# An attention and feed-forward kernel: own score buffers for the first block's head pairs, shared with the first weight tiles, and ten memsets on another engine

## The chip, the cores and the metric

The kernel runs on one core of one Trainium2 chip. A core has a matrix engine (TensorE, PE in the profile, its weight loads PEld), a vector engine (VectorE, DVE), a scalar engine (ScalarE, ACT), a general engine (GpSimd, POOL) and a queue that here issues all transfers (SyncE, SP). Matrix results land in PSUM, everything else lies in SBUF. The metric is the device time of one execution in microseconds (us), as a median of runs.

## What is computed

The reference, cut to what matters; the inputs are float32, and q, k, v and w_in are scaled so that the softmax is far from flat.

```python
# q, k, v: (8 batches, 8 heads, 576 positions, 64); w_in (512, 2048), w_out (2048, 512)
scores = np.matmul(q, k.transpose(0, 1, 3, 2)) / np.sqrt(D)
mask = (rel >= 0) & (rel < 64)            # rel: position of q less position of k
scores = np.where(mask, scores, -1e9)
attn = softmax(scores)
x = np.matmul(attn, v)                    # heads side by side: (4608, 512)
h = x @ w_in
g = np.maximum(h, 0.0) + np.log1p(np.exp(-np.abs(h)))   # softplus
out = g @ w_out                           # (4608, 512)
```

## The kernel before

The 4608 tokens are worked off in 12 blocks of 384 (three tiles of 128). The first two blocks in `ORDER` are the first of their kind, called block 0 and block 1 here, and have an attention of their own in float32 (`by_pe`); the ten others split their operands into high and low parts. A block's attention goes over four pairs of heads. For a pair, SP loads q and k (L204, L206; `kbd` is a block-diagonal key tile whose zeros are memset once) and v (L226, L229); PE multiplies (L254); DVE scales, masks and takes the minimum (L265) into the score buffer `st` and merges the two ends of the window (L271); ACT takes six exponentials (L275); DVE normalises (L280, L281, L283); PE transposes (L290) and multiplies with v (L347); ACT and DVE leave the result as a high and a low part `x` (L352, L353). `st` has two buffers, so pair 2 takes the buffer of pair 0.

The feed-forward part goes over 16 slices of 128 hidden units. `ffn_up` multiplies x with a slice of w_in in twelve products (L401), ACT and DVE form the softplus in L405 to L407 and L409 and split it into `g` (L411, L412), and `ffn_down` adds the slice's nine products with w_out (L422) into three PSUM banks. Block 0 runs slices 0 to 7 first and leaves its partial sums in a DRAM tile `part` (L441, L442); block 1 then runs all 16 slices, block 0 the other eight, and blocks 2 to 11 follow. Block 2's attention lies beside block 1's feed-forward part.

The weights arrive as 64-bit words, 8 KB per partition for a slice of both matrices (1 MB), and are converted on the chip by `load_w`: a transfer into `raws` (L166), ACT (L170), three DVE instructions (L171, L172, L173) in `ws`, two ACT casts that give the high parts (L176) and two POOL subtractions that give the low parts (L177). The buffers of `raws` and `ws` are in the pool `late` under the tags `spare0` to `spare7`; slices 0 to 11 take them in turn. Slices 12 to 15 go through half tiles `raw` and `wh` instead; `raw` is also the buffer through which the partial sums leave.

The order of the work is set twice. `CONVERT`, `BASE`, `PACE` and `STG0` are due times, by which the program emits stages: a pair of block 0 takes its eight stages at `BASE[0] + PACE[0] * hp` plus an offset of `STG0`, so the loads of q and k at -104.5, -99.5, -94.5 and -89.5, and the normalisation and transposes at -96, -91, -86 and -81; the weights of slice f are emitted at `CONVERT[f]`. Then a scheduler places the emitted instructions on each engine by its own timing model, in another order than emitted where it finds that one ready first. From due time 100 on PE's order alone is the emitted one. Each engine, and SP's queue of transfers, works in order.

Of the kernel before, what the change touches and what calls it, by code (L numbers as in the profile page):

```python
# [8 lines left out]
F32 = mybir.dt.float32  # L9
# [6 lines left out]
P = 128  # L16
TB = 384
NJ = TB // P
WIN = 64
BIG = 1.0e9  # L20
CH = 64
# [1 line left out]

SPLIT = 8
DOWN = 5.5
CONVERT = (-104, -98, -93, -88, -6, -3, 0, 3, 6, 8, 11, 13, 16, 18, 21, 24)
BASE = (-100, -10, 24)
PACE = (5, 4, 7)
STG0 = (-4.5, 0.5, 1, 2, 3, 4, 7, 8)
# [10 lines left out]
def window_attention_softplus_ffn(  # L40
# [24 lines left out]
    nc = tc.nc  # L65
# [13 lines left out]
    att = ctx.enter_context(tc.tile_pool(name="att", bufs=1))  # L79
# [12 lines left out]
    NE = NF // 2  # L92
    w_first = [[cpool.tile([P, NE, DM], F32R, name=f"w{m}{i}") for i in range(2)] for m in range(2)]
    w_last = {}

    def spare(k, shape, dtype, name):
        return late.tile(shape, dtype, name=name, tag=f"spare{k}")

    def weight(m, i, f):

        if f < NE:
            return w_first[m][i][:, f, :]
        k = (f - NE) // 4
        if (m, i, k) not in w_last:
            w_last[m, i, k] = spare(4 * k + 2 * m + i, [P, 4, DM], F32R, f"w{m}{i}{k}")
        return w_last[m, i, k][:, f % 4, :]


    W = CH + P
# [2 lines left out]

    kbd_s = [att.tile([P, 2, CH + TB], F32, name="kbd", tag=f"k{i}") for i in range(2)]
    for t in kbd_s:
        nc.gpsimd.memset(t[D:P, 0, :], 0.0)
        nc.gpsimd.memset(t[0:D, 1, :], 0.0)
        nc.gpsimd.memset(t[0:D, 0, 0:CH], 0.0)
        nc.gpsimd.memset(t[D:P, 1, 0:CH], 0.0)

    v13 = cpool.tile([P, NCH, 2, 2, D], BF16, name="v13")  # L120
    v_ts = [att.tile([P, 2, NJ, P], F32, name="v_t", tag=n) for n in ("nat", "tr")]
    for t in v_ts:
        nc.gpsimd.memset(t[0:CH, 0, 0, :], 0.0)

# [23 lines left out]
    def load_w(f):  # L150


        if f < NE + 4:
            k = (0, 4, 2, 6)[f % 4] if f < NE else (4, 6)[f % 2]
            parts = [(spare(k, [P, 2, DM], w_words.dtype, "raws"), spare(k + 1, [P, 2, DM], F32, "ws"), 0, 2)]
        else:
            parts = [
                (
                    ff.tile([P, 1, DM], w_words.dtype, name="raw"),
                    att.tile([P, 1, DM], F32, name="wh", tag=("v_in", "v12")[m]),  # L160
                    m, m + 1,
                )
                for m in range(2)
            ]
        for raw, w, m0, m1 in parts:
            nc.sync.dma_start(raw, w_words[f][:, m0:m1, :])  # L166
            words = raw.bitcast(U32).rearrange("p m (n two) -> p two m n", two=2)
            low, high = words[:, 0, :, :], words[:, 1, :, :]
            wb = w.bitcast(U32)
            nc.scalar.activation(w, high.bitcast(F32), AF.Abs, scale=REBIAS)  # L170
            nc.vector.tensor_scalar(wb, wb, 3, None, ALU.logical_shift_left)  # L171
            nc.vector.scalar_tensor_tensor(wb, high, 0x80000000, wb, ALU.bitwise_and, ALU.bitwise_or)  # L172
            nc.vector.scalar_tensor_tensor(wb, low, 29, wb, ALU.logical_shift_right, ALU.bitwise_or)  # L173
            for m in range(m0, m1):
                hi, lo = [weight(m, i, f) for i in range(2)]
                nc.scalar.copy(hi, w[:, m - m0, :])  # L176
                nc.gpsimd.tensor_tensor(lo, w[:, m - m0, :], hi.bitcast(F32), ALU.subtract)  # L177
# [5 lines left out]
    def attention(g, hp):  # L183
# [59 lines left out]
            nc.vector.tensor_tensor(k_lo, k_in, k_hi.bitcast(F32), ALU.subtract)  # L243
        yield

        st = att.tile([P, 2, NJ, W], F32, name="st", bufs=2)
        mn = att.tile([P, 2, NJ], F32, name="mn", bufs=2)
        sm = att.tile([P, 2 * NJ], F32, name="sm", bufs=2)
        for j in range(NJ):
# [12 lines left out]
            t = ORDER[g] * NJ + j  # L262
# [192 lines left out]
    for g in range(NB):  # L455
        for hp in range(NP):
            if g < 3:
                base = BASE[g] + PACE[g] * hp
            else:
                base = 2 * NF * (g - 1) + SHP * hp + SH  # L460
            stages = attention(g, hp)
            for at in STG if g >= 2 else STG0:
                events.append((base + at, lambda stages=stages: next(stages, None)))
    loaded = 0
    for n, (g, f, first, last) in enumerate(steps):
        if f == loaded:
            events.append((CONVERT[f], lambda f=f: load_w(f)))
            loaded += 1
        events.append((2 * n + 0.5, lambda g=g, f=f: ffn_up(g, f)))
        events.append((2 * n + DOWN, lambda step=steps[n]: ffn_down(*step)))  # L470
# [52 lines left out]
```

## Time and profile before

| | us |
|---|---|
| median of three runs | 1030.87 (1030.74 to 1031.98) |
| the profiled execution | 1030.02 |
| its span, first to last instruction | 1028.2 |
| PE busy | 974.8 (95%) |
| DVE busy | 802.6 (78%) |
| ACT busy | 742.0 (72%) |
| POOL busy | 61.8 (6%) |

The profiled execution's own time is 1.8 us more than its span, for what lies around the instructions, and 0.85 less than the median. The shares are means over the whole span. POOL works only in the first fifth of it, and PE's idle time lies in its first sixth for the most part, so the rows further down are of that part.

### The profile page before, as it was taken

The numbers are of one execution on the slowest core, as the hardware profiler recorded it, in microseconds if no ns is written. First come the engines' busy times: TensorE is split into PE (matmuls) and PEld (weight loads), VectorE is DVE, ScalarE is ACT, GpSimd is POOL, SyncE is SP. The second block draws the span as 40 slices with busy tenths as digits, with TensorE's granted clock in tenths as the row PEclk, the third lists the DMA queues.
The fourth block names the chain that finished last, engine by engine and source line by source line (L and its number), as shares of the span: only waits on it lengthen the run. The fifth ranks groups of instructions, "written<-read, shape, count | busy, mean of one in ns | idle before, by whom it ended". The sixth has DMA issues, their size and how long they took to land.

```text
span 1028.2 us, 16614 instructions
## 1 busy us (share of the span) xinstructions
PE 974.8 (95%) x5888; PEld 859.1 (84%) x5888; DVE 802.6 (78%) x1775; ACT 742.0 (72%) x1705; POOL 61.8 (6%) x56
## 2 busy tenths in 40 slices
PE   4559889999999999999999999999999999999998
PEld 2337778988888998998899899899989899889997
DVE  6998587797987888878878878878878887874332
ACT  5467477787877788778778778778878877865443
POOL 5365020000000000000000000000000000000000
PEclk8679989999999999999999999999999999999999
DMA  8662253375554456444444534534634635521000
GB/s 295 229 219 71 88 149 83 83 186 123 126 121 114 113 114 130 117 113 116 131 103 117 140 91 118 151 83 113 164 83 113 161 86 104 141 49 32 31 1 31
DMA packets 203155, 119.05 MB, mean 116 GB/s; under 512 B 130880, under 2 KB 195136, under 8 KB 201536
## 3 DMA queue, kind: packets, MB, share of 16 engines
q1 hardware_dynamic: 203072, 118.00, 45.4%
q8 instruction: 46, 0.75, 0.3%
q14 instruction: 37, 0.30, 0.1%
HBM read 76.28 MB, written 10.22 MB: 84 GB/s over the span
## 4 chain that ended last, share of the span: by engine, by line
PE 85%; DVE 9%; DMA 2%; ACT 1%; issue 1%; SPq 1%; DVEq 0%; ACTq 0%
PE ps_o L422 37%; PE ps_h L401 37%; PE ps_a L376 5%; PE ps_a L258 5%; DVE ws L172 2%; DVE ws L173 1%; DVE st L265 1%; DVE st L283 1%; DMA raws<-in_w_words_dram 1%; DVE ws L171 1%; DVE st L271 0%; DMA tr<-nat 0%; ACT st L275 0%; PE ps_a L254 0%; DVE sm L280 0%
## 5 line engine op out<-in xcount | busy, mean ns | idle before, releaser
L401 PE MATMUL ps_h<-x,w 128*128 128x384 f32 x2304 | 445.3, 340 | 7.6 <-ACT x L352 3.9
L422 PE MATMUL ps_o<-w,g 128*128 128x512 f32 x1728 | 435.5, 395 | 0.0
L401 PEld LDWEIGHTS ps_h<-x,w 128*128 128x128 f32 x2304 | 402.6, 189 | 22.5 <-ACT x L352 5.2
L422 PEld LDWEIGHTS ps_o<-w,g 128*128 128x128 f32 x1728 | 318.0, 188 | 57.7 <-ACT g L411 0.3
L405 ACT ACTIVATE u<-ps_h 128x384 f32<-128x384 f32 x192 | 93.9, 490 | 121.8 <-PE ps_h L401 118.8
L409 DVE SCALAR_TENSOR_TENSOR u<-ps_h,u 128x384 f32<-128x384 f32 x192 | 106.4, 554 | 70.5 <-ACT u L407 69.2
L275 ACT ACTIVATE st<-st,mn 128x128 f32<-128x128 f32 x288 | 111.9, 390 | 19.3 <-DVE st L271 19.3
L412 DVE TENSOR_TENSOR g<-u,g 128x384 fp32r<-128x384 f32 x192 | 106.6, 555 | 10.5 <-ACT g L411 8.6
L265 DVE CUSTOM_DVE_ANT_0 st<-ps_a,mask 128x192 f32<-128x192 f32 x216 | 69.4, 351 | 57.9 <-PE ps_a L258 45.4
L407 ACT ACTIVATE u<-u 128x384 f32<-128x384 f32 x192 | 100.3, 523 | 4.2
L406 ACT ACTIVATE u<-u 128x384 f32<-128x384 f32 x192 | 100.7, 526 | 3.2
L258 PE MATMUL ps_a<-k,q_hl 128*128 128x192 f32 x480 | 76.5, 283 | 0.0
L376 PEld LDWEIGHTS <-v 128*128 128x128 bf16 x1088 | 56.1, 98 | 22.9 <-issue 21.8
L376 PE MATMUL ps_a<-tr,v 128*128 128x128 bf16 (+1 forms) x1088 | 72.0, 213 | 0.2
L258 PEld LDWEIGHTS ps_a<-k,q_hl 128*128 128x128 f32 x480 | 66.6, 192 | 4.1 <-issue 0.5
L411 ACT CAST g<-u 128x384 fp32r<-128x384 f32 x112 | 57.0, 509 | 14.2 <-DVE u L409 13.5
L306 ACT CAST nat<-st 128x768 bf16<-128x768 f32 x40 | 33.2, 831 | 40.0 <-DVE st L304 40.0
L275 ACT ACTIVATION_READ_ACCUMULATOR st<-st,mn 128x1 f32 x288 | 53.9, 187 | 0.0
L381 ACT COPY xf<-ps_a 64x384 f32<-64x384 f32 x80 | 38.1, 477 | 20.3 <-PE ps_a L376 19.2
L283 DVE TENSOR_TENSOR st<-st,sm 128x768 f32<-128x768 f32 x48 | 47.6, 991 | 1.5
L382 DVE TENSOR_TENSOR xf<-ps_a,xf 64x384 f32<-64x384 f32 x80 | 43.9, 548 | 5.2 <-ACT xf L381 4.0
L325 DVE TENSOR_TENSOR v_in<-v_in,v 128x896 f32<-128x896 f32 x40 | 43.5, 1086 | 4.7 <-ACT v L324 4.7
(80 smaller groups left out, 868.0 us busy)
## 6 DMA issues: line engine op xcount, KB each, us to landing
k_in<-in_kT_dram SPq DMA_DIRECT2D x80, 224.0 KB, 3.9
v_in<-in_v_dram SPq DMA_DIRECT2D x80, 224.0 KB, 3.6
q_in<-in_qT_dram SPq DMA_DIRECT2D x84, 192.0 KB, 4.1
raws<-in_w_words_dram SPq DMA_DIRECT2D x12, 1024.0 KB, 6.0
out_dram<-raw SPq DMA_DIRECT2D x12, 512.0 KB, 2.8
raw<-in_w_words_dram SPq DMA_DIRECT2D x8, 512.0 KB, 4.3
out_dram<-raw SPq DMA_DIRECT2D x12, 256.0 KB, 2.6
v_t<-in_v_dram SPq DMA_DIRECT2D x16, 96.0 KB, 3.8
```

Of the source, the lines that this page charges most:

```text
L258: mm(spv[:, hh, :], q_hl[:, hh, js], part[:, hh, kc], start=(hh == 0 and i == 0), stop=(hh == 1 and i == 1), skip_group_check=True,)
L265: nc.vector.tensor_tensor_reduce(st[:, hh, j, :], spv[:, hh, :], m, QSCALE, 3.0e38, ALU.add, ALU.min, mn[:, hh, j : j + 1])
L275: nc.scalar.activation(sv[:, i, 0:P], sv[:, i, 0:P], AF.Exp, bias=mn[:, hh, j : j + 1], scale=-1.0, accum_out=sm[:, i : i + 1])
L283: nc.vector.tensor_tensor(pn, pn, sm.unsqueeze(2).to_broadcast([P, 2 * NJ, P]), ALU.mult)
L376: mm(av[:, osl], (v13 if s else v12)[:, c, hh, :, :], src, start=(i == 0), stop=(i == len(passes) - 1), skip_group_check=True,)
L401: mm(hv, weight(0, a, f)[:, c * P : (c + 1) * P], x[b][c], start=(i_mm == 0), stop=(i_mm == 3 * NC - 1))
L405: nc.scalar.activation(u, hv, AF.Abs)
L406: nc.scalar.activation(u, u, AF.Exp, scale=-1.0)
L407: nc.scalar.activation(u, u, AF.Ln, bias=1.0)
L409: nc.vector.scalar_tensor_tensor(gf, hv, 0.0, u, ALU.max, ALU.add)
L412: nc.vector.tensor_tensor(gt[1], gf, gt[0].bitcast(F32), ALU.subtract)
L422: mm(ops[g][j], gt[a][:, js], weight(1, b, f), start=(first and i == 0), stop=(last and i == 2),)
```

## The change

It does three things. The ten memsets of `kbd` and `v_t` go from POOL to DVE. In block 0, each pair's score buffer is now a tile `st0` of its own, placed under the tags `spare0`, `spare4`, `spare2` and `spare6`, which the words of slices 0 to 3 take afterwards. And the due times of the first four weight slices go from -104, -98, -93 and -88 to -95.5, -90.5, -85.5 and -80.5, half a unit behind the normalisation and the transposes of the pair whose buffer they take.

```diff
-CONVERT = (-104, -98, -93, -88, -6, -3, 0, 3, 6, 8, 11, 13, 16, 18, 21, 24)
+CONVERT = (-95.5, -90.5, -85.5, -80.5, -6, -3, 0, 3, 6, 8, 11, 13, 16, 18, 21, 24)
...
+    FIRST = (0, 4, 2, 6)
...
-        nc.gpsimd.memset(t[D:P, 0, :], 0.0)
-        nc.gpsimd.memset(t[0:D, 1, :], 0.0)
-        nc.gpsimd.memset(t[0:D, 0, 0:CH], 0.0)
-        nc.gpsimd.memset(t[D:P, 1, 0:CH], 0.0)
+        nc.vector.memset(t[D:P, 0, :], 0.0)
+        nc.vector.memset(t[0:D, 1, :], 0.0)
+        nc.vector.memset(t[0:D, 0, 0:CH], 0.0)
+        nc.vector.memset(t[D:P, 1, 0:CH], 0.0)
...
-        nc.gpsimd.memset(t[0:CH, 0, 0, :], 0.0)
+        nc.vector.memset(t[0:CH, 0, 0, :], 0.0)
...
-            k = (0, 4, 2, 6)[f % 4] if f < NE else (4, 6)[f % 2]
+            k = FIRST[f % 4] if f < NE else (4, 6)[f % 2]
...
-        st = att.tile([P, 2, NJ, W], F32, name="st", bufs=2)
+        if g == 0:
+
+            st = spare(FIRST[hp], [P, 2, NJ, W], F32, "st0")
+        else:
+            st = att.tile([P, 2, NJ, W], F32, name="st", bufs=2)
```

Since the scheduler decides, the order itself shows what moved. The line numbers after the change are 2 higher up to L238 and 6 higher from L260 on. SP's queue from its start before (`raws` takes a whole slice's words, `k_in` and `q_in` hold q, `kbd` holds k):

```order
L204 DMA k_in_124<-in_qT_dram 128x384
L206 DMA kbd_89<-in_kT_dram 64x384 x2
L166 DMA raws_128<-in_w_words_dram 128x1024
L229 DMA v_t_100<-in_v_dram 64x128
L226 DMA v_t_100<-in_v_dram 128x2x128
L226 DMA v_t_100<-in_v_dram 64x3x128 x2
L204 DMA q_in_143<-in_qT_dram 128x384
L206 DMA kbd_90<-in_kT_dram 64x384 x2
L166 DMA raws_158<-in_w_words_dram 128x1024
```

And after, from the second pair's v on:

```order
L231 DMA v_t_101<-in_v_dram 64x128
L228 DMA v_t_101<-in_v_dram 128x2x128
L228 DMA v_t_101<-in_v_dram 64x3x128 x2
L206 DMA k_in_187<-in_qT_dram 128x384
L208 DMA kbd_89<-in_kT_dram 64x384 x2
L206 DMA q_in_259<-in_qT_dram 128x384
L208 DMA kbd_90<-in_kT_dram 64x384 x2
L168 DMA raw_983<-in_w_words_dram 128x512
L168 DMA raw_985<-in_w_words_dram 128x512
L168 DMA raws_172<-in_w_words_dram 128x1024
```

The first whole slice (`raws_128`, now `raws_172`) goes from the fourth transfer to behind q and k of all four pairs and behind two half tiles of slice 12. DVE from the end of pair 1's scores before:

```order
L271 TENSOR_TENSOR st_202<-st_202 128x6x64
L171 TENSOR_SCALAR ws_159<-ws_159 128x1024
L280 TENSOR_SCALAR sm_149<-sm_149 128x6
L172 SCALAR_TENSOR_TENSOR ws_159<-raws_158,ws_159 128x1024
L281 RECIPROCAL sm_149<-sm_149 128x6
L173 SCALAR_TENSOR_TENSOR ws_159<-raws_158,ws_159 128x1024
L283 TENSOR_TENSOR st_147<-st_147,sm_149 128x6x128
L280 TENSOR_SCALAR sm_204<-sm_204 128x6
L281 RECIPROCAL sm_204<-sm_204 128x6
L171 TENSOR_SCALAR ws_223<-ws_223 128x1024
L283 TENSOR_TENSOR st_202<-st_202,sm_204 128x6x128
```

And after:

```order
L277 TENSOR_TENSOR st0_191<-st0_191 128x6x64
L286 TENSOR_SCALAR sm_138<-sm_138 128x6
L287 RECIPROCAL sm_138<-sm_138 128x6
L289 TENSOR_TENSOR st0_136<-st0_136,sm_138 128x6x128
L286 TENSOR_SCALAR sm_193<-sm_193 128x6
L297 COPY pt_161<-ps_a_167 128x384
L287 RECIPROCAL sm_193<-sm_193 128x6
L289 TENSOR_TENSOR st0_191<-st0_191,sm_193 128x6x128
L173 TENSOR_SCALAR wh_984<-wh_984 128x512
```

The conversions have gone from between the steps of the two softmaxes; the first that follows is of a half tile. DVE in block 1's feed-forward part, from the 15th to the 18th end of a softplus (u), before:

```order
L409 SCALAR_TENSOR_TENSOR u_1326<-ps_h_1313,u_1326 128x384
L304 TENSOR_TENSOR st_1378<-st_1378,nat_1502 128x6x128
L311 COPY nat_1502<-nat_1502 128x12x64
L412 TENSOR_TENSOR g1_1332<-u_1326,g0_1331 128x384
L310 TENSOR_TENSOR nat_1502<-st_1378,nat_1502 128x12x64
L409 SCALAR_TENSOR_TENSOR u_1364<-ps_h_1351,u_1364 128x384
L412 TENSOR_TENSOR g1_1370<-u_1364,g0_1369 128x384
L409 SCALAR_TENSOR_TENSOR u_1429<-ps_h_1416,u_1429 128x384
```

And after, from shortly ahead of the 16th to the 17th:

```order
L418 TENSOR_TENSOR g1_1332<-u_1326,g0_1331 128x384
L310 TENSOR_TENSOR st_1545<-st_1545,nat_1721 128x6x128
L317 COPY nat_1721<-nat_1721 128x12x64
L331 TENSOR_TENSOR v_in_1774<-v_in_1774,v12_1921 128x896
L415 SCALAR_TENSOR_TENSOR u_1364<-ps_h_1351,u_1364 128x384
L335 COPY v13_99<-v12_1921 64x14x64
L286 TENSOR_SCALAR sm_1766<-sm_1766 128x6
L287 RECIPROCAL sm_1766<-sm_1766 128x6
L289 TENSOR_TENSOR st_1764<-st_1764,sm_1766 128x6x128
L316 TENSOR_TENSOR nat_1721<-st_1545,nat_1721 128x12x64
L334 TENSOR_TENSOR v13_99<-v_in_1774,v12_1921 64x14x64
L418 TENSOR_TENSOR g1_1370<-u_1364,g0_1369 128x384
```

Instructions of block 2's attention (names with st, nat, v_in, v12, v13) that stood behind these softplus ends stand ahead of them now.

## Rows read from the trace of the kernel before

**Rows 1.** Busy time of the engines by stretch of the span: start and end in us, length, then busy us and instructions of each engine, TensorE's granted clock as a share of full speed, busy share of the DMA engines, GB/s.

```profile
0.00:7.56 7.56, 3.06 (x5) 1.85 (x6) 0.00 (x1) 1.28 (x1) 6.51 (x24) 1.00 0.70 213
7.56:69.56 62.00, 32.55 (x166) 20.31 (x164) 60.32 (x117) 34.41 (x86) 29.78 (x17) 0.72 0.75 253
69.56:123.67 54.11, 47.07 (x264) 38.12 (x265) 40.85 (x89) 34.21 (x90) 18.64 (x12) 0.94 0.27 82
123.67:134.94 11.27, 5.67 (x41) 4.70 (x39) 5.40 (x11) 5.13 (x18) 0.00 (x0) 0.85 0.65 218
134.94:160.00 25.06, 23.16 (x114) 20.21 (x114) 24.75 (x56) 21.69 (x47) 6.84 (x4) 0.93 0.59 139
160.00:219.00 59.00, 58.77 (x360) 52.46 (x361) 43.12 (x98) 45.71 (x109) 0.00 (x0) 1.00 0.40 95
...
300.00:500.00 200.00, 200.00 (x1258) 179.47 (x1257) 167.45 (x384) 156.79 (x358) 0.00 (x0) 1.00 0.52 120
```

The columns of engines are PE, PEld, DVE, ACT and POOL.

**Rows 2.** PE's waits in the first 100 us: PE's line, the engine and line waited for, us in total, times, the longest.

```profile
PE ps_a L290 <- DVE st L283: 16.2, 3, 10.6
...
PE ps_o L254 <- DVE x L353: 4.8, 1, 4.8
```

**Rows 3.** The chain of work that ended last, in order of time, around the end of the first pass: start, us, what.

```profile
124.13 0.59 ACT raw L441
124.75 3.61 DMA part<-raw
128.38 3.58 DMA raw<-in_w_words_dram
132.04 0.67 ACT wh L170
133.19 0.70 DVE wh L172
133.91 0.69 DVE wh L173
```

**Rows 4.** The first instruction of L409, from DVE's timeline: start, us, engine, line, what.

```profile
78.79 0.55 DVE L409 SCALAR_TENSOR_TENSOR u<-ps_h,u 128x384 f32<-128x384 f32 x1
```

**Rows 5.** DVE's timeline in two stretches in which its instructions follow each other without a gap; a price is the distance from one start to the next.

```profile
81.42 0.34 DVE L265 CUSTOM_DVE_ANT_0 st<-ps_a,mask 128x192 f32<-128x192 f32 x1
...
81.69 0.35 DVE L265 CUSTOM_DVE_ANT_0 st<-ps_a,mask 128x192 f32<-128x192 f32 x1
...
81.97 0.68 DVE L171 TENSOR_SCALAR ws<-ws 128x1024 uint32<-128x1024 uint32 x1
82.57 0.54 DVE L412 TENSOR_TENSOR g<-u,g 128x384 fp32r<-128x384 f32 x1
83.04 1.21 DVE L173 SCALAR_TENSOR_TENSOR ws<-raws,ws 128x1024 uint32<-128x1024 uint32 x1
84.17 0.54 DVE L412 TENSOR_TENSOR g<-u,g 128x384 fp32r<-128x384 f32 x1
...
150.16 0.17 DVE L280 TENSOR_SCALAR sm<-sm 128x6 f32<-128x6 f32 x1
150.36 0.19 DVE L281 RECIPROCAL sm<-sm 128x6 f32<-128x6 f32 x1
150.59 0.96 DVE L283 TENSOR_TENSOR st<-st,sm 128x768 f32<-128x768 f32 x1
151.46 0.55 DVE L412 TENSOR_TENSOR g<-u,g 128x384 fp32r<-128x384 f32 x1
```

**Rows 6.** POOL's subtractions in the first 135 us, by line and form: count, busy us, mean ns of one, idle time before them and what ended it.

```profile
L177 POOL TENSOR_TENSOR w<-ws,w 128x512 fp32r<-128x512 f32 x24 | 41.9, 1768 | 42.1 <-ACT w L176 42.1
```

**Rows 7.** The tile `raws`, by line: count, duration in ns (least, median, most), first and last start; and the time from issue to landing of its transfers.

```profile
L170 ACT ACTIVATE ws<-raws x12: 1106/1139/1166, 9.2 to 79.7; 128x1024 f32<-128x1024 f32 x12
L172 DVE SCALAR_TENSOR_TENSOR ws<-raws,ws x12: 1212/1669/2294, 11.5 to 85.1; 128x1024 uint32<-128x1024 uint32 x12
...
DMA to landing us min/median/max: 4.8/6.0/11.0
```

**Rows 8.** The timeline of the first 12 us: POOL's first memset of `kbd`, the first transfer of words, POOL's first mask, PE's products of pair 0, POOL's last mask, DVE's first score reduction, PE's products of pair 1.

```profile
0.73 0.47 POOL L115 MEMSET kbd<- 64x448 f32 x1 [0.29 <-POOLq L509]
...
2.43 0.59 SPq L166 DMA_DIRECT2D raws<-in_w_words_dram  x1
...
3.52 0.26 POOL L129 MEMSET mask<- 128x192 bf16 x1
...
4.50 4.18 PE L254 MATMUL ps_a<-kbd,k_in 128*128 128x384 f32 x6 [4.50 <-DMA kbd<-in_kT_dram]
...
7.24 0.20 POOL L145 MEMSET mask_b<- 64x128 bf16 x1
...
7.56 0.36 DVE L265 CUSTOM_DVE_ANT_0 st<-ps_a,mask 128x192 f32<-128x192 f32 x1 [7.56 <-POOL mask_b L145]
...
11.40 3.58 PE L254 MATMUL ps_o<-kbd,q_in 128*128 128x384 f32 x6 [2.72 <-DMA kbd<-in_kT_dram]
```

**Rows 9.** The timeline of the softmaxes of pairs 0 and 1: two of ACT's exponentials that follow each other, DVE's two multiplications.

```profile
13.66 0.39 ACT L275 ACTIVATE st<-st,mn 128x128 f32<-128x128 f32 x1
...
14.04 0.39 ACT L275 ACTIVATE st<-st,mn 128x128 f32<-128x128 f32 x1
...
20.65 2.03 DVE L283 TENSOR_TENSOR st<-st,sm 128x768 f32<-128x768 f32 x1
...
25.52 0.94 DVE L283 TENSOR_TENSOR st<-st,sm 128x768 f32<-128x768 f32 x1
```

**Rows 10.** The chain of work again, in block 1's feed-forward part: the products of three groups in a full stretch.

```profile
174.99 2.13 PE ps_h L401 x12
177.11 2.08 PE ps_o L422 x9
...
183.47 2.10 PE ps_h L401 x12
```

## The prediction

> **What bounds the kernel now.** I read the busy time by stretch first, since the page's shares mix a front of some 160 us with 870 us in which PE is full. From 0 to 134.94 us VectorE (DVE) is busy 0.00 + 60.32 + 40.85 + 5.40 = 106.6 us and idle 28.4 us; from 160 to 219 us PE is busy all but 0.2 us of 59, and from 300 to 500 all of it [rows 1]. So only the front can change, and the change touches only the front. There PE's long waits are for DVE: 16.2 us for the softmax's multiplication (L283) and 4.8 us for an x (L353) [rows 2]. The chain says the same: between the end of the first FFN pass (L441) and the last x of block 1 (L353 at 134.94) it runs through the spilled partial sums, the reload of `raw` and DVE's conversion of a half weight tile, which stands ahead of that x on DVE [rows 3].
>
> DVE's idle time lies in four places: 7.56 us at the start, 1.68 us up to 69.56 (the last x of block 0), 13.26 us up to 123.67 (the first L441), 5.87 us up to 134.94 [rows 1]. The third is the prize: there PE works off the first pass and DVE has nothing ready, having converted ten weight tiles before PE had a first slice finished (first L409 at 78.79 [rows 4]).
>
> **The change, part by part.** Prices of DVE instructions are spacings of instructions that follow each other without a gap [rows 5]: L171 0.60, L172 and L173 1.13 each where nothing disturbs (2.86 for a conversion of a whole tile), 0.275 for a score reduction, 0.47 for L409, L412, L353 and their like; of a softmax, L280 0.20, L281 0.23 and the multiplication L283 0.87.
>
> Counted with these along the order, DVE's work up to the last x of block 1 is the same before and after: 12 conversions 34.3, 48 reductions 13.2, eight times L271, L280, L281, L283, L291 and L353 together 21.7, eight slices' L409 and L412 7.5, half tiles 8.0 and the rest 2.2, 86.9 us. The trace spends 106.6, so 19.7 us are stretching. I put it down to POOL's subtractions (24 of 1.77 us beside these conversions [rows 6]): L172 takes 1.21 at least and 2.29 at most [rows 7]. Both orders run the same subtractions beside the same conversions, so I keep 19.7. The Trainium skill (SBUF — State Buffer, Who interferes with whom) says that a VectorE instruction with two SBUF inputs and a GpSimd one that reads SBUF exclude each other, and that the second waits for the whole of the first. The trace bears out the direction; were all 24 waits whole, they would be 42 us and not 19.7, and the sum below would lose 23, which L172's longest row, 1.08 above its shortest, speaks against.
>
> *The memsets.* POOL's ten take from 0.73 to 3.52, and its masks from there until 7.44, when DVE starts [rows 8]. Without the ten, the masks are ready 2.8 earlier, at 4.7. Then PE is late next: its first products begin at 4.50, when the keys have landed, and take 4.18 for six, 1.4 for the pair of a tile, so DVE starts near 6.0, not 7.56: 1.6 saved. The trace has no memset on DVE; between half of POOL's price and twice it (1.4 to 5.6) they end at 2.1 to 6.3; I take POOL's price, 3.5, inside DVE's wait, and the long end costs 0.3.
>
> *Weights after the scores.* SP now issues both first heads' loads and v before any weight tile. The second pair's keys landed at 11.40 behind 1 MB of words issued at 2.43 [rows 8]; now near 9. The softmaxes of pairs 0 and 1 meet neither conversions nor POOL: pair 0's scores end near 9.3, its six exponentials (0.38 apart [rows 9]) near 12.3, pair 1's near 15.6, the two multiplications at 14.5 and 17.8, where they end at 22.7 and 26.5 now [rows 9]. In those 8 us DVE has 4.4 of work: idle 3.5, and about 1 for the first half tile. The first weight's load waits for pair 0's transposes at 16.1, and with 6.0 to landing [rows 7] and ACT's 1.1 DVE can convert from 23.5; by then it is still at its 13th us of counted work, near 24.7, so this wait is hidden (if pair 0 is late, it is paid one for one). The later loads queue on SP behind the loads of v, k and q, and the order has slices 4 and 5 converted ahead of 2 and 3, since the last two wait for pairs 2 and 3. I find no stop above 1 us in that.
>
> *PE is fed earlier.* Ahead of the first L409 stand 54.0 us of counted work before, 39.1 after. By the count, from 13.0 at 24.7 with 1.3 of stretching per conversion, the last x of block 0 comes near 50 (69.56 now) and the first L409 near 58 (78.79). PE then needs DVE's conversions and not the reverse; its eight slices take 8 x (2.13 + 2.08) [rows 10] = 33.7, and the last L441 follows DVE's 82.2nd us of work. So the 13.26 us of idle in the third place shrink to X, stalls on ACT's chain (L405 to L407, L411) and on exponentials. Bounds: 0 and 13.3. The nearest row is DVE with a backlog from 7.56 to 69.56, idle 1.68 in 62 [rows 1], which is 1.6 for these 60 us; I take 3, since products and softplus now depend on each other there.
>
> *The chain after the first pass* (spill, reload, half tile: 3.61 + 3.58 + 0.67 and DVE's part [rows 3]) is not touched: 5.87 stays.
>
> Up to the last x of block 1: saved 1.6 + 1.7 + (13.3 - 3.0), lost 4.5 and about 1 of new stops: 8 us, so 127 and not 134.94.
>
> *What is given back.* From that x on the new order has DVE do block 2's attention ahead of the softplus of block 1. To the 14th L409 it has 34.0 of counted work (24.5 before), to the 17th 49.8 (31.7 before). With 3 of stretching the 14th ends 37 after that x; PE, held to two slices of L401 ahead, may by then have done five slices of both kinds (21.0), the ends of two and of block 1's attention (1.9) and 7.2 of block 2's products, 30.1 together by its order, so it idles 7. Before, 47.0 of work, counted in the same way up to the 20th slice's L401, took 185.57 - 134.94 = 50.6 [rows 10]: 3.6. The loss is 3.5: part of what DVE does earlier also puts PE's products for block 2 earlier (7 us by the 18th slice), and that is not lost. Bounds: 0, if PE has no gap that it hadn't, and 18.1 - 6.5 = 11.6, DVE's extra work to the 17th less PE's own extra.
>
> Net 8.0 - 3.5 = 4.5 us. From the profiled execution's 1030.02 that is 1025.5; the median of the runs shown lies 0.85 above that execution, so **1026**.
>
> **The rivals.**
> *Slower: block 2's attention ahead of block 1's softplus.* Place: from the last x of block 1, on DVE. If DVE is the bound there throughout, the loss is 11.6, and with only 8 gained by then the time is 1030.9 + 3.6 = 1034.5. It decides against the change once PE's idle time after that x grows by more than what that x has gained. For it: DVE is busy 24.75 of 25.06 us there already [rows 1]. Against it: PE can run two slices ahead, and DVE's backlog ends by the 20th slice, where PE's own work has caught up.
> *No gain: the freed idle time comes back as waits.* X is 7 to 9, because DVE's in-order queue now meets conversions whose words wait for a transposition, and products that wait for the conversion: 8 - 5 - 3.5, nothing, 1030.5. For it: DVE waited 13.3 in that stretch; against it: the 1.68 before.
> *More: X near 1 and no loss after.* 8 + 2 - 0, 1021. For it: the backlog lasts to the end of the first pass.
> *The change doesn't do what it says*: DVE stands still on the first weight because pair 0's transposes are not early. Each us late is a us lost; counted in the second rival.
>
> **How the numbers follow.** The forecast (1022 to 1029 around 1026) gets 0.42, the larger gain 0.16, no gain 0.20, slower 0.22. The range must leave out no more than 2 in 10: down to 1019 (the larger gain, with 2 us less stretching), up to 1035 (the slower rival). What a measurement can tell here is about 0.2%, 2.1 us: faster means under 1028.8. The forecast lies mostly below that, so faster 0.42 x 0.93 + 0.16 + a fifth of the no-gain case: 0.59; within 0.2% the rest of these, 0.19; slower 0.22.
>
> **What would show it.** Right: DVE's first score near 6.0, the multiplications of pairs 0 and 1 near 14.5 and 17.8, no wait over 1 us before the first L171 on a whole tile, the last x of block 0 near 50, the first L409 near 58, some 3 us of idle time on DVE from the last x of block 0 to the first L441, the last x of block 1 near 127, and PE idle about 7 us in the 40 us after. Wrong: an L172 or L170 that waits several us for words in 25 to 50 us (the second rival), a last x of block 1 later than 131, or PE waits for L409 after it that add up to more than 8 us (the first).

## The result, and the profile after

The changed kernel takes 1038.6 us (median of 4 runs, 1037.06 to 1038.74) against 1031.4 (1030.74 to 1032.73) for the kernel before, run beside it: a ratio of 1.0068, with a 95% interval from 1.0056 to 1.008. It is slower by about 7 us; 1026 was forecast, 1019 to 1035 as the range. (One execution of run 11 below took 1215 us at a granted clock of 0.745 and is left out of its median and interval.) The profiled execution took 1038.66, its span 1036.4; PE is busy for 980.6 us of it (974.8 before), DVE for 806.9 (802.6).

The busy time by stretch of the kernel after, with ends chosen to answer [rows 1]: first score, last x of block 0, first L447 (before: L441), last x of block 1, and two places further on. Columns as in [rows 1].

```profile
0.00:6.29 6.29, 1.78 (x3) 1.17 (x4) 2.41 (x11) 1.28 (x1) 3.95 (x14) 1.00 0.39 114
6.29:51.33 45.04, 30.47 (x168) 19.41 (x166) 37.75 (x98) 24.37 (x70) 9.91 (x6) 0.81 0.86 275
51.33:119.62 68.29, 52.18 (x272) 41.54 (x273) 66.51 (x108) 44.92 (x106) 33.16 (x22) 0.88 0.40 129
119.62:129.99 10.37, 3.77 (x35) 3.05 (x33) 5.23 (x12) 4.68 (x17) 1.25 (x1) 0.76 0.67 223
...
160.00:219.00 59.00, 56.95 (x333) 50.13 (x331) 38.84 (x83) 43.27 (x95) 0.00 (x0) 0.97 0.34 79
252.00:320.00 68.00, 64.15 (x411) 54.71 (x410) 59.39 (x139) 52.24 (x119) 0.00 (x0) 1.00 0.59 137
```

The front did what was forecast in kind: DVE's backlog, 1.68 us of idle time in 62 before [rows 1], now lies from 51.33 to 119.62 with 1.78 of idle time in 68.29, and the last x of block 1 comes at 129.99, 4.95 earlier than before. But PE, full from 160 on before, is idle for 2.05 us up to 219 and for 3.85 from 252 to 320, where the kernel before has no gap:

```profile
252.00:320.00 68.00, 68.00 (x433) 60.33 (x433) 57.59 (x131) 52.72 (x120) 0.00 (x0) 1.00 0.51 114
```

DVE's timeline has the steps that the prediction named (start, us):

```profile
6.29 0.36 DVE L271 CUSTOM_DVE_ANT_0 st<-ps_a,mask_c 128x192 f32<-128x192 f32 x1 [2.50 <-PE ps_a L260]
...
13.05 0.96 DVE L289 TENSOR_TENSOR st<-st,sm 128x768 f32<-128x768 f32 x1
...
15.95 0.96 DVE L289 TENSOR_TENSOR st<-st,sm 128x768 f32<-128x768 f32 x1
...
51.33 0.54 DVE L359 TENSOR_TENSOR x<-ps_o,x 128x384 fp32r<-128x384 f32 x1
...
60.10 1.01 DVE L415 SCALAR_TENSOR_TENSOR u<-ps_h,u 128x384 f32<-128x384 f32 x2
```

The last of these answers [rows 4]: the first softplus end comes 18.7 us earlier (60.10 for 78.79). Of that lead 5 us are left at the last x of block 1; the 13th end still comes 1.7 earlier (157.97 for 159.63), the 14th already 5.7 later (168.81 for 163.14), and from the 51st (351.79 for 343.62) to the last the kernel is 8.2 us late without a change. Between the 13th and the 14th end the timeline of DVE and PE reads:

```profile
157.97 0.55 DVE L415 SCALAR_TENSOR_TENSOR u<-ps_h,u 128x384 f32<-128x384 f32 x1
...
163.10 1.08 DVE L245 TENSOR_TENSOR k<-k_in,k 128x896 fp32r<-128x896 f32 x1
164.04 0.32 PE L382 MATMUL ps_a<-tr,v 128*128 128x128 bf16 x3
164.10 0.55 DVE L418 TENSOR_TENSOR g<-u,g 128x384 fp32r<-128x384 f32 x1
164.19 2.31 PE L428 MATMUL ps_o<-w,g 128*128 128x512 f32 x9
164.68 0.96 DVE L239 TENSOR_TENSOR q_hl<-q_in,q_hl 64x768 fp32r<-64x768 f32 x1
165.67 0.55 DVE L388 TENSOR_TENSOR xf<-ps_a,xf 64x384 f32<-64x384 f32 x1
166.14 1.07 DVE L331 TENSOR_TENSOR v_in<-v_in,v 128x896 f32<-128x896 f32 x1
166.34 1.03 PE L264 MATMUL ps_a<-k,q_hl 128*128 128x192 f32 x8
167.14 0.38 DVE L335 COPY v<-v 64x896 bf16<-64x896 bf16 x1
167.44 0.94 DVE L316 TENSOR_TENSOR nat<-st,nat 128x768 bf16<-128x768 f32 x1
168.53 0.36 DVE L271 CUSTOM_DVE_ANT_0 st<-ps_a,mask 128x192 f32<-128x192 f32 x1
168.81 0.55 DVE L415 SCALAR_TENSOR_TENSOR u<-ps_h,u 128x384 f32<-128x384 f32 x1
...
169.42 0.99 PE L407 MATMUL ps_h<-x,w 128*128 128x384 f32 x2 [2.05 <-DVE u L415]
```

All of DVE's rows between the two L415 but the L418 are block 2's attention. PE has done what it can by 167.37 and stands until DVE reaches the softplus end: in that time DVE is busy throughout with work that PE does not need next. In the part that is left out, DVE itself waited twice for block 2's attention, 1.76 us for its scores on PE and 0.56 for ACT; since its instructions stand in one order, the softplus end waited too.

How far ahead that work stands is read from the two orders: so many DVE instructions of later blocks' attention (blocks 2 and up) stand ahead of the n-th softplus end in the whole kernel (the 9th is the first of block 1).

| kernel | 14th | 20th | 28th | 34th | 42nd | 51st |
|---|---|---|---|---|---|---|
| before | 29 | 40 | 96 | 122 | 164 | 211 |
| after | 48 | 77 | 93 | 130 | 187 | 211 |

There are two places, one up to the 25th end and a second around the 42nd; from the 51st on the orders are the same, where the loss stops growing.

### The profile page after: what moved, and what is told of

It reads as the page before. It is cut to its first block, busy times and chain, and to the rows that moved or that the text cites. A ratio compares the mean times of both kernels' runs of the same rounds, so it can differ in the third digit from the quotient of the medians.

```text
span 1036.4 us, 16632 instructions
## 1 busy us (share of the span) xinstructions
PE 980.6 (95%) x5888; PEld 863.9 (83%) x5888; DVE 806.9 (78%) x1785; ACT 741.4 (72%) x1705; POOL 55.2 (5%) x46
## 4 chain that ended last, share of the span: by engine, by line
PE 79%; DVE 9%; DMA 6%; ACT 3%; issue 2%; SPq 1%; ACTq 0%; DVEq 0%
PE ps_h L407 35%; PE ps_o L428 34%; PE ps_a L382 5%; PE ps_a L264 5%; DMA tr<-nat 2%; DMA raws<-in_w_words_dram 2%; DVE ws L175 1%; DVE ws L174 1%; DMA raw<-in_w_words_dram 1%; DVE st L271 1%; DVE g L418 1%; DVE u L415 1%; DVE k L245 1%; DVE st L277 1%; DMA v_in<-in_v_dram 0%
## 5 line engine op out<-in xcount | busy, mean ns | idle before, releaser
L407 PE MATMUL ps_h<-x,w 128*128 128x384 f32 x2304 | 451.9, 344 | 24.9 <-DVE u L415 13.5
L407 PEld LDWEIGHTS ps_h<-x,w 128*128 128x128 f32 x2304 | 409.3, 192 | 42.4 <-ACT w L178 14.9
L415 DVE SCALAR_TENSOR_TENSOR u<-ps_h,u 128x384 f32<-128x384 f32 x192 | 106.2, 553 | 79.1 <-ACT u L413 77.9
L281 ACT ACTIVATE st<-st,mn 128x128 f32<-128x128 f32 x288 | 111.9, 390 | 18.9 <-DVE st L277 18.8
L418 DVE TENSOR_TENSOR g<-u,g 128x384 fp32r<-128x384 f32 x192 | 109.3, 569 | 12.4 <-ACT g L417 10.4
L417 ACT CAST g<-u 128x384 fp32r<-128x384 f32 x112 | 56.9, 509 | 18.9 <-DVE u L415 17.8
L387 ACT COPY xf<-ps_a 64x384 f32<-64x384 f32 x80 | 38.1, 476 | 19.9 <-PE ps_a L382 18.7
L289 DVE TENSOR_TENSOR st<-st,sm 128x768 f32<-128x768 f32 x48 | 49.7, 1036 | 1.4
```

Source lines behind the costliest of these rows:

```text
L281: nc.scalar.activation(sv[:, i, 0:P], sv[:, i, 0:P], AF.Exp, bias=mn[:, hh, j : j + 1], scale=-1.0, accum_out=sm[:, i : i + 1])
L407: mm(hv, weight(0, a, f)[:, c * P : (c + 1) * P], x[b][c], start=(i_mm == 0), stop=(i_mm == 3 * NC - 1))
L415: nc.vector.scalar_tensor_tensor(gf, hv, 0.0, u, ALU.max, ALU.add)
L417: (nc.scalar.copy if g < 2 or f % 2 else nc.vector.tensor_copy)(gt[0], gf)
L418: nc.vector.tensor_tensor(gt[1], gf, gt[0].bitcast(F32), ALU.subtract)
```

## The experiments

In the first eight and one of the last three kernels an engine's instructions are held to a written order: a list names them, and each is made to follow the one ahead of it on its engine. What the list doesn't name (SP and POOL too, where not said otherwise) is placed by the scheduler. The first 167 DVE instructions, up to the last x of block 1 and without the memsets, are the same set before and after, so a front can be joined to the other kernel's tail. Marks are starts in the profiled run: last x of block 1, 28th and 54th softplus end (slice 11 of block 0, slice 5 of block 3, counted from 0).

| kernel | last x | 28th | 54th | ratio to before (95%) |
|---|---|---|---|---|
| before | 134.94 | 231.64 | 356.19 | |
| after | 129.99 | 232.37 | 364.36 | 1.0068 (1.0056 to 1.008) |
| 1 new front, old tail | 129.48 | 226.17 | 351.37 | 0.9952 (0.994 to 0.9964) |
| 2 old front, new tail | 136.15 | 238.28 | 371.12 | 1.0136 (1.0123 to 1.0149) |
| 3 memsets alone | 136.05 | 232.76 | 358.05 | 1.0007 (0.9999 to 1.0016) |
| 4 after, memsets on POOL | 127.82 | 229.41 | 361.04 | 1.0054 (1.0038 to 1.007) |
| 5 new order up to the 28th, then old | 129.34 | 231.12 | 363.26 | 1.0058 (1.0045 to 1.0071) |
| 6 as 1, last x ahead of half tile | 129.24 | 228.58 | 353.57 | 0.9957 (0.9943 to 0.9971) |
| 7 old tail on DVE alone | 129.25 | 230.59 | 355.72 | 0.9993 (0.9985 to 1.0002) |
| 8 old buffers, new order | 127.75 | 229.01 | 361.26 | 1.0044 (1.0032 to 1.0056) |
| 9 after, constant 60 | 128.03 | 229.34 | 355.31 | 1.0008 (0.9999 to 1.0017) |
| 10 after, constant 32 | 128.05 | 228.68 | 353.79 | 0.9971 (0.996 to 0.9982) |
| 11 after, constant 20 | 130.35 | 228.91 | 354.03 | 0.9964 (0.9951 to 0.9977) |
| 12 before, constant 32 | 134.16 | 230.72 | 356.17 | 0.9996 (0.9988 to 1.0005) |
| 13 old buffers, new front, old tail | 128.61 | 225.39 | 350.37 | 0.994 (0.9928 to 0.9953) |
| 14 due times alone, constant 32 | 138.33 | 235.73 | 360.87 | 1.0039 (1.0026 to 1.0052) |
| 15 after, memsets on POOL, constant 32 | 126.52 | 224.89 | 350.38 | 0.9944 (0.993 to 0.9958) |

**Fronts and tails exchanged (1, 2).** The edit to the changed kernel (1); 2 is the same on the kernel before, with the changed kernel's list:

```diff
+HELD = {
+    "DVE": """
+A1.3.7:0 W14:4 A2.0.1:0 W14:5 A2.0.3:0-2 W15:0 U1.0:0 A2.0.4:0-2 W15:1 U1.1:0 A2.0.5:0-2 A2.1.2:0 W15:2 U1.0:1 A2.1.1:0 A2.0.6:0 W15:3 U1.1:1 W15:4
...
+    for _engine, _text in HELD.items():
+        _hold(_engine, _text)
```

(`A2.0.3` is stage 3 of block 2's pair 0, `W14` the conversion of slice 14, `U1.0` the `ffn_up` of block 1's slice 0.)

> The changed kernel, with PE, ACT and DVE held to the order of the kernel before from the last x of block 1 on (the same 167 DVE instructions stand up to that x in both kernels, so the two tails can be exchanged whole); ahead of that x all is as in the changed kernel. The last x of block 1 came 4.95 us earlier after the change (129.99 against 134.94), and from there to the end the changed kernel lost 13.1. Theory (the front gained, the later order that the scheduler made lost it): some 4 to 5 us faster than before, 1026 to 1028. Rival (the x is early, but PE's work is not: counted in nominal matmul time PE stood only 0.9 us ahead at 144 us, so the front itself had used up its lead): 1030 to 1032. Second rival (the loss is made by the front, whatever order follows): 1036 or more.

> The kernel before, with PE, ACT and DVE held to the order of the changed kernel from the last x of block 1 on. Theory (the later order loses whatever the front was): 1038 to 1044, up to 13 us slower than before. Rival (the loss comes out of the front, the later order is harmless): 1031 to 1033.

Measured 1025.74 and 1044.89, beside 1030.65 for the kernel before. The front gains 4.9 us, the tail loses 12 to 14 behind either front. From the last x to the 28th end and on to the 54th, the windows of the kernel after:

```profile
129.99:232.37 102.38, 96.78 (x536) 85.77 (x537) 76.73 (x172) 77.80 (x181) 6.99 (x4) 0.92 0.48 112
232.37:364.36 131.99, 128.14 (x785) 111.90 (x784) 105.80 (x236) 98.25 (x224) 0.00 (x0) 1.00 0.53 119
```

and of the new front with the old tail:

```profile
129.48:226.17 96.69, 96.56 (x548) 86.13 (x549) 79.35 (x177) 78.02 (x182) 6.89 (x4) 0.95 0.49 121
226.17:351.37 125.20, 124.34 (x773) 109.36 (x772) 103.76 (x231) 98.57 (x223) 0.00 (x0) 1.00 0.55 123
```

The loss is 5.7 us in the first place and 6.8 in the second. DVE's busy time differs by no more than 2.6 in either pair of rows, once to each side; PE's idle time differs by more (5.60 for 0.13, 3.85 for 0.86). In the second place PE's busy time is 3.8 longer too. Twelve more matmuls in the stretch are a part of that; the rest is waiting that the rows count as busy. A product of 128x512 is drawn 398 ns long in this stretch, but the next mostly starts 231 ns after it, so a wait shows only with what outlasts the drawn end. Measured from start to start, and against the median spacing of each shape of product, PE's products here take 8.6 us longer in all, and 2.7 in run 9 (below), which has the same 785; ten waits between 262 and 310 us make 5.5 of the difference of 5.9.

**Memsets (3, 4).** The kernel before with `nc.vector.memset` for the ten, and the changed kernel with them back on POOL, all five engines held:

```diff
-        nc.gpsimd.memset(t[D:P, 0, :], 0.0)
+        nc.vector.memset(t[D:P, 0, :], 0.0)
...
```

> The kernel before with the ten memsets on DVE, all engines held to the order of before. The prediction's term: the first score at 6.0 instead of 7.56, and 1.6 us saved up to the last x of block 0, where DVE has a backlog. If that is carried to the end, 1029.8; if the idle time of DVE ahead of the first end of a pass (13 us) swallows it, 1031.4, no change.

> The changed kernel with the ten memsets back on POOL, all engines held to the order of the changed kernel. If the moved memsets are worth their 1.6 us in the changed front (DVE busy nearly throughout from 20 to 82 us), 1040.2; if the later waits swallow it, 1038.6.

Measured 1031.78 and 1035.56. The moved memsets save nothing. DVE's first score in the kernel of run 3:

```profile
7.41 0.36 DVE L353 CUSTOM_DVE_ANT_0 st<-ps_a,mask 128x192 f32<-128x192 f32 x1 [3.62 <-PE ps_a L342]
```

The masks are done at 4.64 there, but the order of before takes a tile whose products PE ends only then: 0.15 saved. In the changed order the first score does come earlier, 6.29 with the memsets moved and 7.19 with them on POOL, but PE's products of pair 0 take until 8.7 and the last of its scores starts at 9.01 and at 8.99.

**The second place (5).** The changed kernel, its own order to the 28th end, then the old one:

> The changed kernel with its own order up to the 28th end of a softplus (slice 12 of block 0, near 232 us) and from there the order of the kernel before on PE, ACT and DVE. Against the kernel with the new front and the old tail (1025.7) the changed one is 0.5 us behind at the last x of block 1, 6.2 behind at the 28th end and 13.0 at the 54th. If the loss has these two places and each comes from the order there: 6.8 us less than the changed kernel, 1032. Rival (the second half only follows from the first, DVE being behind at 232 us): 1038.

Measured 1036.52, near the rival; but the run doesn't tell. From its 30th end at 246.10 to the 54th it takes 117.2 us, as the old tail does from its own 30th end on (116.3; the new one 122.2), so the old order is good there too. Going from one order to the other costs what that saves: in the 15 us up to 246.10 PE is busy for 11.46, at a clock of 0.77, and waits 3.2 for one score that the old order has much earlier. Run 9 asks the same without a jump.

**The last x ahead of the half tile (6).** The order on DVE, as such a list; on ACT alike:

```diff
-A1.3.5:1-5 W14:0-4 A1.3.7:0 W14:4 A2.0.1:0
+A1.3.5:1-5 A1.3.7:0 W14:0-5 A2.0.1:0
```

> New front and old tail as in the run above that gave 1025.7, with one move: the last x of block 1 (ACT's copy and DVE's subtraction) ahead of the half tile of slice 14 on both engines. There PE ends the products of that x at 127.0, and the copy waits until 128.88 behind two conversions of words that landed at 126.65 and 128.31. If the half tile is what holds block 1's feed-forward part: the x at 127.6 instead of 129.5 and 1.9 us saved, 1023.8. Rival (the half tile's own weights, or DVE's queue, are needed next anyway): 1025.7.

Measured 1025.37: the rival. (The profiled execution is a long one, 1027.87, and its front lies later: the products of that x end at 128.70, so that the x comes at 129.24 all the same.) The x no longer waits behind the half tile, but what PE has next, block 2's scores, does:

```profile
129.24 0.56 DVE L435 TENSOR_TENSOR x<-ps_a,x 128x384 fp32r<-128x384 f32 x1 [2.54 <-ACT x L434]
129.26 2.29 PE L483 MATMUL ps_h<-x,w 128*128 128x384 f32 x6 [0.57 <-ACT x L434]
...
132.79 1.91 DVE L315 TENSOR_TENSOR q_hl<-q_in,q_hl 64x768 fp32r<-64x768 f32 x1
...
134.85 2.84 PE L340 MATMUL ps_a<-k,q_hl 128*128 128x192 f32 x12 [3.30 <-DVE q_hl L315]
```

PE's wait of 2.4 for the x has become one of 0.6 for the x and 3.30 for block 2's q behind the half tile.

**DVE alone (7), and the buffers (8).** 7 keeps only the list of DVE from run 1; 8 is the kernel before with all engines held to the changed order.

> The changed kernel with DVE alone held to the order of before from the last x of block 1 on; PE and ACT are placed by the scheduler. If DVE's order (block 2's and block 3's attention ahead of softplus ends) is the cause: 1026, as with all three held. Rival (PE's or ACT's order has its own share): 1030 or more.

> The kernel before, its two score buffers and its memsets on POOL kept, with all five engines held to the order of the changed kernel. If the four buffers free no wait of their own in that order (pair 2's scores come behind pair 0's transposes there anyway) and only let the scheduler find it: the time of the changed order with the memsets on POOL, 1035.6. Rival (pair 2 needs its own buffer in this order): 1038 or more.

Measured 1029.99 and 1035.02. Beside 1030.32 for the kernel before and 1025.74 for run 1: DVE's order makes some 8 of the 12 to 13 us, those of PE and ACT the other 4. And in the changed order two score buffers do as well as six (1.0044; 1.0054 in run 4, with the own ones): the own buffers take no wait away by themselves.

**One constant (9 to 12).**

```diff
-PE_ORDERED_FROM = 100
+PE_ORDERED_FROM = 60
```

From this due time on PE's order is the emitted one; DVE and ACT, which follow PE's products, can then run less far ahead. 10 and 11 have 32 and 20, 12 is the kernel before with 32.

> The changed kernel with one constant changed: PE's emitted order holds from due time 60 on, not from 100. DVE's order is word for word that of the changed kernel up to the 28th end of a softplus; behind it the scheduler no longer puts block 3's attention ahead (161 instead of 187 DVE instructions of later attention stand ahead of the 42nd end; 164 before the change). So this takes away the second place alone, without a jump from one order to the other. Against the kernel with the old tail the changed one loses 5.7 us from the last x of block 1 to the 28th end and 6.8 from there to the 54th. If the second place stands by itself: 6 to 7 us less than the changed kernel, 1031.5 to 1032.5. Rival (the second loss only follows from the first, as the jump at 232 us that gave 1036.5 allowed): 1036 or more.

> The changed kernel with PE's emitted order from due time 32 on: both places are taken away by one constant (24, 39 and 161 DVE instructions of later attention ahead of the 14th, 20th and 42nd end, against 48, 77 and 187 after the change and 29, 40 and 164 before it). Theory (the front gains, the order behind it lost it): as with the old tail, 1025 to 1027. Rival (the old tail was good by its own details, not by holding the attention back): 1030 or more.

> The same from due time 20 on, which holds block 2's attention back further in the first place (17, 39 and 161 ahead of the 14th, 20th and 42nd end; 29, 40 and 164 before the change). If only attention that stands too early costs: 1025 to 1027 as with 32. Rival (its products on PE then wait for DVE later): 1 to 4 us more than with 32.

> The kernel before with the same constant, 32: the control. Both kernels then have nearly the same order behind the 14th end, so the pair shows what the change is worth by itself. Theory: the constant does nothing here (the order before was already of this kind), 1029 to 1032, and the change is worth 4 to 6 us. Rival (the constant helps both kernels alike): 1025 to 1027, and the change is worth nothing.

Measured 1032.27, 1027.79, 1027.5 and 1030.53, beside 1030.93 for the kernel before. With 60, whose DVE order is the changed kernel's up to the 28th end, the first place is as slow as after the change and the second is gone:

```profile
128.03:229.34 101.31, 95.27 (x536) 83.52 (x537) 76.53 (x173) 77.72 (x181) 6.30 (x4) 0.95 0.47 115
229.34:355.31 125.97, 125.13 (x785) 112.30 (x784) 105.27 (x235) 98.51 (x224) 0.00 (x0) 1.00 0.54 123
```

So the second place stands by itself: 6 us (125.97 for 131.99), and by the ratios as much (1.0008 for 1.0068). It has 785 matmuls as the changed kernel's stretch, in 125.13 of busy time and not 128.14. With 32 the first place is eased too, though not gone (100.63 us from the last x to the 28th end, 96.69 with the old tail), so the time is a little above what was expected. What is left of that place lies at its start: 8 and 11 instructions of block 2's attention stand ahead of the 9th and 10th softplus end with 32 as after the change (4 and 6 before), and PE waits 2.42 us for the first of them (2.40 after the change, 0.93 before). With 20 the time is that of 32, so holding back still more neither gains nor costs. The constant does nothing to the kernel before; beside it the change is worth 1030.5 - 1027.8 = 2.7 us, where 4 to 6 were expected.

**Which part of the change makes the gain (13 to 15).** 13 is run 8 with the order of run 1; 14 is the kernel before with the new `CONVERT` and constant 32; 15 is run 10 with the memsets on POOL.

> The kernel before, with its two score buffers and its memsets on POOL, all five engines held to the order of the run that gave 1025.7 (new front, old tail). If the gain is the order alone (the conversions behind the softmaxes), 1025 to 1026. If the own buffers or the moved memsets carry the 1.6 and 1.7 us that the prediction gave to the start: 1027 to 1029.

> The kernel before with the new due times of the first four conversions alone, and PE's emitted order from due time 32 on; the scheduler places the rest. If the due times are what the front's gain needs: about as the whole change with that constant, 1027 to 1029. If without the four buffers the scheduler's front stays as it was: 1030 to 1031.

> The changed kernel with the ten memsets back on POOL and PE's emitted order from due time 32 on. By the prediction's term for the memsets 1.6 us more than with them moved, 1029.4; if they are worth nothing, as the pair with held orders says, 1026 to 1028.

Measured 1024.44, 1034.72 and 1024.62, beside 1030.75. The gain is the order alone: with the old buffers and the memsets on POOL it is 6.3 us. But the scheduler does not find that order from the new due times alone: without the four buffers its front gets worse (last x at 138.33), which neither expectation had. The four buffers with the old due times were not tried. In all four pairs the moved memsets lean to a cost: 0.7 us by the ratio in run 3, 1.4 in the changed kernel against 4, 1.2 in 1 against 13 (which has the old buffers too), 2.8 in 10 against 15. In the first three the intervals overlap or touch no change, and in the last the scheduler's order differs as well; no wait in the traces shows why.

## Why the prediction was wrong

*What bounds the kernel*: right for the kernel before. "Only the front can change" was wrong: it is a statement on PE under the order of before, and the change gave a new order to some 350 us.

*The memsets*: the first score at 6.29 is as forecast (6.0). The 1.6 us weren't there, since PE's products end the pair (runs 3 and 4): that term is 0, or below.

*Weights after the scores*: right in the main. The multiplications come at 13.05 and 15.95 (14.5 and 17.8 forecast). DVE waited 2.71 for the first half tile's words and 1.63 ahead of a whole tile, where no stop above 1 was forecast behind the first.

*PE is fed earlier*: right, x at 51.33 (50), first L415 at 60.10 (58), X, DVE's idle time, 1.8 (3). *The chain after the first pass*: 10.37 in all (11.27 before). That the last x came at 129.99 and not at 127 is mostly stretching: DVE was busy for 2.41 + 37.75 + 66.51 + 5.23 = 111.9 us up to it, where 86.9 of counted work and 19.7 of stretching had been put; without the 2.4 ahead of the first score, mostly memsets, 22.6 and not 19.7. What stretches it was not tested. What the front gains to the end was sized at 8; it measured 4.9 (run 1).

*What is given back* is the step that failed. It was put at 3.5, with 11.6 as the most; it measured 12 to 13. Its mechanism was right, and so was its place as far as it went: 7 us of idle time on PE in the 40 us after the last x were forecast, and 5.6 are there.

```profile
130.00:140.00 10.00, 7.57 (x26) 6.71 (x27) 9.90 (x24) 8.44 (x17) 3.50 (x3) 0.50 0.50 144
140.00:150.00 10.00, 10.00 (x52) 9.17 (x51) 9.91 (x27) 9.63 (x26) 3.49 (x2) 0.89 0.62 134
150.00:160.00 10.00, 8.88 (x56) 7.97 (x54) 8.42 (x21) 5.62 (x18) 0.00 (x0) 1.00 1.03 168
160.00:170.00 10.00, 7.95 (x58) 6.85 (x57) 8.95 (x22) 9.28 (x23) 0.00 (x0) 0.97 0.66 145
```

Of the 5.6, 4.4 are two waits for L415 and 1.1 one for the transfer that transposes block 2's attention (`tr` from `nat`). The kernel before, from its last x to the 28th end:

```profile
134.94:231.64 96.70, 94.56 (x548) 83.72 (x549) 79.44 (x178) 78.14 (x182) 6.84 (x4) 0.98 0.50 123
```

It is idle for 2.1 us, so the idle time grew by 3.5, as was put; but the stretch grew by 5.7. The other 2.2 are busy time (96.78 for 94.56, with twelve matmuls fewer) at a mean granted clock of TensorE of 0.92 and not 0.98. In 130 to 140 us the clock was 0.50, the lower of its two levels, after 10.37 us in which PE was busy for 3.77. The sum had no term for the clock. Run 1, with the old order and the same 548 matmuls, shows that price without the waits: 96.56 of busy time at 0.95, for 94.56 at 0.98.

The larger part was missed because the count stopped at the 20th softplus end, where DVE's extra work was to have been worked off. The order puts block 3's attention ahead a second time from the 32nd end on, and that cost 6 to 7 more (6.0 against run 9, 6.8 against run 1), in a stretch in which PE had no gap before. The orders showed it; the prediction read them only around the place that it had in mind. Its signs of being wrong did not tell either: the last x came ahead of 131, and PE's waits for L415 behind it add up to 4.4 in the first place, not to 8.

*The rivals*: "slower" named the mechanism, at 1034.5 with the price of the first place alone. Runs 1, 2 and 9 show the cause as far as the order goes, run 7 that DVE's part is the larger. "The change doesn't do what it says" is half true: the buffers take away no wait in that order. That they change what the scheduler finds ready first is the likely reading of run 14; no run shows it by itself. Why its model puts the attention ahead, and whether it puts it there for the 5 us of lead, wasn't tried.

## What to carry to other kernels

Where a scheduler places the work, an edit is priced by the whole new order, not by the stretch in which the lines stand: compare the orders until they are the same again, and count on each engine how much work of later stages stands ahead of the work that the bound engine waits for. To tell an edit from the order that it happens to give, hold the order and exchange front and tail; a gain of 5 us and a loss of 12 lay in one result of 7. What cured it here was to hold back what runs ahead, not to give up the new front: the changed kernel with its memsets on POOL and one constant is 0.56% faster than the kernel before (0.9944, 0.993 to 0.9958).

## What the runs showed that was not expected

The landing of the first words varies between runs, and DVE's backlog carries it on: with one order on DVE in the changed kernel and in run 9, the changed kernel is 1.2 us behind from the first half tile on and 2.0 from 44 us to the last x. The order on PE and ACT is the same too up to 232 us, and SP issues the first half tile's words at 13.02 and 13.05; ACT starts on them at 18.93 and at 17.73:

```profile
18.93 0.66 ACT L172 ACTIVATE wh<-raw 128x512 f32<-128x512 f32 x1 [3.41 <-DMA raw<-in_w_words_dram]
```

```profile
17.73 0.66 ACT L172 ACTIVATE wh<-raw 128x512 f32<-128x512 f32 x1 [2.17 <-DMA raw<-in_w_words_dram]
```

The last x of block 1 comes at 129.99 and at 128.03. So a mark in the front, read from one profile, is good to 2 us; the lengths of the stretches behind it agree better, and the medians decide.
